# Lending shift adds from VectorE to GpSimd, with two more rules that vary by stretches

## The chip, the cores and the metric

The kernel runs on one core of one Trainium2 chip. The metric is the device time of one execution in microseconds (us); the median of several executions is compared. A profile is one execution recorded by the hardware: busy spans of TensorE (PE, with its weight loads as PEld), VectorE (DVE), ScalarE (ACT) and GpSimd (POOL), the transfers, and what each instruction waited for.

## What is computed

The program is four blocks on a sequence of 2048 rows of 512 numbers: attention, mixer with MLP, attention, mixer with MLP, each with a layer norm before it and a residual sum after it. The attention has 32 query heads of width 16 and one shared key and value head:

```python
def _A_ref(x, wq, wk, wv, wo):
    q = (x @ wq).reshape(B, S, H, Dh).transpose(0, 2, 1, 3)
    k = x @ wk
    v = x @ wv
    scores = jnp.einsum("bhqd,bkd->bhqk", q, k) * (Dh ** -0.5)
    p = _softmax(scores, axis=-1)
    o = jnp.einsum("bhqk,bkd->bhqd", p, v)
    return o.transpose(0, 2, 1, 3).reshape(B, S, H * Dh) @ wo
...
x = x + _A_ref(_layernorm(x, axis=-1), A_wq, A_wk, A_wv, A_wo)
x = x + _B_ref(_layernorm(x, axis=-1), B_w1, B_w2, B_w3, B_w4)
x = x + _A_ref(_layernorm(x, axis=-1), A_wq, A_wk, A_wv, A_wo)
x = x + _B_ref(_layernorm(x, axis=-1), B_w1, B_w2, B_w3, B_w4)
```

The mixer block `_B_ref` normalises, multiplies by w1, applies gelu, shifts four groups of channels by one or two rows up or down, multiplies by w2, and then runs a normalised MLP with w3, gelu and w4. The exponentials are the bulk of the elementwise work: 2 layers of 32 x 2048 x 2048 scores.

## The kernel before

**The work.** Queries are handled in chunks of 512 (the last one of the second layer is cut into two of 256), heads in 8 blocks of four, keys in 16 blocks of 128. A *half* is two heads' scores of one chunk against 128 keys (or, in a chunk of 256, against 256 keys): 1024 columns on 128 partitions, two PSUM banks. There are 2048 halves in all.

**Two ways for a half.** As a *unit* (`declare_unit`, line 1171) PE makes the scores with two matmuls into two neighbouring banks, and ACT writes exp of them to a slot of EA with one instruction (line 1186). As a *pair* (`declare_pair`, line 1194) the same two tiles are evicted by VectorE, one at a time (line 1206): an affine map to uint16 whose bits, read as bfloat16, are close to the exponential. Such an approximation is made three times with different offsets and averaged: the second and third rows come out of the row before by adding a constant to the integers (the *shift add*, line 1243 in `shift_op`), and each of the three rows goes through its own weighted value matmul. J has N_J = 5 slots of three rows.

**The chain of shift adds.** When pair m is declared, one two-row instruction makes the third row of pair m-1 and the second row of pair m (`shift`, line 1224). So each such instruction reads a row that the one before it wrote. Where a block of heads ends with a pair pending, a one-row instruction finishes it (`finish_pair`).

**Who does a shift add.** It is declared for GpSimd if the rows pending there are fewer than ADDS, else for VectorE. When VectorE has nothing to do, `borrow` (line 288) lets it take a ready shift add out of GpSimd's heap, if GpSimd is busy.

**The order.** The whole order of instructions is made in Python by an event-driven plan (`Plan`) with assumed durations. Each engine has a heap of operations; when it comes free, `_pick` takes the ready one with the lowest key of priority and sequence: 0 for unit scores, 1 for VectorE's evictions, 2 for value matmuls and shift adds, 10 for most token work (norms, projections, MLP). The result is a fixed instruction list for each engine, with semaphore waits between them. `assign` (line 1480) decides when a half becomes a pair: only if few pairs are in flight (MAX_PAIRS), VectorE's queue is short (QUEUE), its side work is small (BACKLOG), and a slot of J is free.

**Early score tiles.** `coming` (line 350) computes when ACT will need each unit's scores; they are urgent LEAD (0.4 us) before the last moment, with an allowance for switching PE from another kind of matmul. A unit that isn't urgent yet may be attached to a run of score matmuls that is going on, with the key JOIN (1.3), so ahead of value matmuls (2).

**The clock guess.** The plan assumes that PE runs fast while its recent activity is above a share: WARM (0.40) to get there, STAY (0.36) to stay there (`roll`, line 197). A filler matmul is put in where the activity would fall short of KEEP.

**Stretches.** `temper` (line 1443) sets the rules named in RULES anew each 12.5 us of planned time: digit w of the string TEMPER (116 digits) names one of 16 rows of MOODS.

Of the kernel before, what the change touches and what calls it, by code (L numbers as in the profile page):

```python
# [15 lines left out]
class Late:  # L16
# [4 lines left out]
    def __init__(self, n=1):  # L21
        self.bank = None
        self.n = n
        self.ops = []
        self.gates = []
# [7 lines left out]
class Plan:  # L33
# [12 lines left out]
    WINDOW = 3.4133  # L46
    BINS = 4
    WARM = 0.40
    STAY = 0.36
    KEEP = 0.55  # L50
    CREDIT = 0.2
    URGENT = 0.6
# [6 lines left out]
    PATIENCE = 3.0  # L59
    SLACK = -0.1  # L60
    DMA_LATE = 2.5
    EAGER = 0.0
# [9 lines left out]
    LEAD = 0.4  # L72
    JOIN = 1.3
    LEFT = 1
    HORIZON = 1.0
    LULL = 0.45

    def __init__(self, nc, pool_banks):
        self.nc = nc
# [117 lines left out]
    def roll(self, t):  # L197
        w = int(t * self.BINS / self.WINDOW)
        while self.window < w:
            ask = self.STAY if self.warm else self.WARM  # L200
            self.warm = sum(self.activity[-self.BINS:]) >= ask * self.WINDOW * 2400.0
# [86 lines left out]
    def borrow(self, t):  # L288

        if self.free_at["POOL"] <= t + 1e-9 or self.port - t > self.LULL:  # L290
            return None
# [5 lines left out]
        o.eng, o.dur, o.after = "DVE", o.flex, 0.0  # L297
        return o

    def deferred(self, h, t, joins):  # L300

        low = {}
        if self.pe_kind != "P":
            ps = [o for o in h if o.pe[0] == "P" and o.prio == 2 and o.ready <= t + 1e-9]
            if len(ps) < self.BUNCH and not any(o.ready < t - self.PATIENCE for o in ps):
                low = {o: self.WAITING for o in ps}
        if not (joins and self.pe_kind == "Q"):
            low.update({o: self.ALONE for o in h if o.prio == 0.5})
        return low
# [148 lines left out]
    def run(self, pump):  # L458
        while True:
            if not self.events:  # L460
                if pump(self.now):
                    continue
                break
            t = heapq.heappop(self.events)
            while self.events and self.events[0] <= t + 1e-9:
                heapq.heappop(self.events)
            self.now = max(self.now, t)
            again = True
            while again:
                again = pump(self.now)  # L470
                for e in ENGINES:
                    if self.free_at[e] <= self.now + 1e-9:
                        o = None
                        if e == "PE" and self.now >= self.pe_end - 1e-9 and self.idle():
                            o = self._pick(e, self.now, dense=True)
                            if o is None:
                                self.filler()
                        if o is None:
                            o = self._pick(e, self.now)
                        if o is None and e == "DVE":  # L480
                            o = self.borrow(self.now)
                        if o is None and e == "PE" and self.now >= self.pe_end - 1e-9 and self.left \
                                and self.filler is not None:
                            heapq.heappush(self.events, self.now + 0.25)
                        if o is not None:
                            self._place(o, self.now)
                            again = True
        if self.left:
            for e in ENGINES:
                for o in self.heap[e][:5]:  # L490
                    print("STUCK", e, o.prio, o.seq, o.take)
            raise AssertionError(f"{self.left} operations never became ready at {self.now}")
# [82 lines left out]
def t_x4(n):  # L575
    return 0.068 + n * 0.26e-3
# [18 lines left out]
class Kernel:  # L595
# [13 lines left out]
    ADDS = 6  # L609
# [12 lines left out]
    MAX_PAIRS = 2  # L622
    BACKLOG = 1
    FAR = 20
    FREE = 1
    LONELY = 3
    SOON = 0.45
    QUEUE = 0.7

    STRETCH = 12.5  # L630
    RULES = ("KEEP", "PATIENCE", "BACKLOG", "LONELY", "SOON", "QUEUE", "MAX_PAIRS", "ADDS", "EAGER")
    MOODS = (
        (0.55, 3.0, 1.0, 3.0, 0.45, 0.7, 2, 6, 0.0),
        (0.53, 2.5, 0.8, 3.0, 0.45, 0.7, 2, 7, 0.0),
        (0.57, 3.5, 1.2, 3.3, 0.45, 0.7, 2, 6, 8.0),
        (0.52, 3.0, 1.5, 2.0, 0.6, 0.7, 2, 7, -6.0),
        (0.55, 2.0, 1.0, 3.0, 0.3, 1.0, 2, 6, 0.0),
        (0.55, 4.0, 0.7, 4.0, 0.45, 0.5, 2, 6, 0.0),
        (0.55, 3.0, 1.0, 3.0, 0.45, 0.7, 1, 6, 20.0),
        (0.55, 3.0, 1.5, 2.5, 0.6, 1.0, 3, 7, -15.0),  # L640
        (0.60, 3.0, 0.6, 3.0, 0.2, 0.4, 2, 6, 0.0),
        (0.50, 2.7, 1.1, 2.8, 0.5, 0.8, 2, 6, 0.0),
        (0.55, 3.0, 1.0, 3.0, 0.45, 0.7, 2, 6, 20.0),
        (0.55, 1.0, 1.0, 3.0, 0.45, 0.7, 2, 6, 0.0),
        (0.55, 3.0, 1.0, 3.0, 0.45, 0.7, 2, 7, 0.0),
        (0.55, 3.0, 1.0, 3.0, 0.45, 0.7, 2, 6, -15.0),
        (0.55, 3.0, 1.5, 3.0, 0.7, 1.2, 3, 8, 0.0),
        (0.57, 2.0, 1.0, 2.0, 0.45, 1.0, 3, 6, 0.0),
    )
    TEMPER = "0184777f99f477e52777e374efe430779ef2771778570177e0083e2004000314093e49710fef799feef443873f1e0ee11705c154031407220200"  # L650

    def __init__(self, nc, ins, out):
        self.stretch = -1
# [585 lines left out]
    def shift_op(self, d, f, rows):  # L1239
        n = len(rows)  # L1240
        self.adds = [p for p in self.adds if not p.placed]
        eng = "POOL" if sum(p.weight for p in self.adds) < self.ADDS else "DVE"
        o = self.pl.op(eng, lambda e: e.tensor_scalar(  # L1243
            out=self.J[:, d, :], in0=self.J[:, f, :], scalar1=float(self.STEP), scalar2=1.0, op0=ALU.add, op1=ALU.mult),
            reads=[t for r in rows for t in self.jtag(r - 1)], writes=[t for r in rows for t in self.jtag(r)],
            dur=t_x4(1024 * n) if eng == "DVE" else 0.264 + 0.859 * n, prio=2, side=False, port=True,
            after=0.0 if eng == "DVE" else 0.07)
        if eng == "DVE":
            self.pairs[-1] = o
        else:  # L1250
            o.weight = n
            o.flex = t_x4(1024 * n)
            self.adds.append(o)

    def add_pv(self, g, es, m=None, done=1):
# [187 lines left out]
    def temper(self, now):  # L1443
# [3 lines left out]
        self.stretch = w  # L1447
        mood = self.MOODS[int(self.TEMPER[w], 36) if w < len(self.TEMPER) else 0]
        for name, v in zip(self.RULES, mood):
            setattr(self.pl if hasattr(self.pl, name) else self, name, v)  # L1450

    def pump(self, now):

        self.temper(now)
        did = False
        n = len(self.halves)
        while True:
            if sum(1 for o in self.units[-4:] if not (o.placed and o.end <= now + 1e-9)) >= 3:
                break
            while self.hi in self.given:  # L1460
                self.hi += 1
            self.pl.closing = self.hi + self.CLOSING >= n
            if self.hi >= n:
                break
            self.hi += 1
            self.declare_unit(self.halves[self.hi - 1])
            did = True
        if now > self.attached + self.LONELY and self.assign(now, self.ndve % 2):
            did = True
        if not self.main_done and self.seg == len(self.segs) \  # L1470
                and all(o.placed for o in self.units[-2:]) and self.last_copy.placed:
            self.main_done = self.pl.loose = True
        return did
# [291 lines left out]
```

## Time and profile before

| What | Value |
|---|---|
| median of 3 runs | 1454.44 us (1454.4 to 1456.4) |
| the profiled execution | 1452.62 us, of which 1450.8 us span from the first to the last instruction |
| PE busy | 1425.7 us (98%), 29716 matmuls |
| VectorE busy | 1321.1 us (91%), 2383 instructions |
| ScalarE busy | 1382.0 us (95%), 1471 instructions |
| GpSimd busy | 1139.6 us (79%), 825 instructions |
| shift adds on GpSimd, on VectorE | 529 (967.2 us), 162 (114.7 us) |
| halves as units, as pairs | 1389, 659 |
| transfers | 21.75 MB, 15 GB/s over the span |

How to read it: busy time is the time in which an engine executes an instruction, as a share of the span. Matmuls overlap, so PE's busy share is not its load. In the rows of groups, a line such as "L1243 POOL TENSOR_SCALAR J<-J" names the line of the kernel, the engine, the operation, and what is written from what; then come the shape, the count, the busy us, the mean ns of one, and the engine's idle us just before, with the instructions that ended them.

### The profile page before, as it was taken

The page shows a single profiled execution, that of the slowest core. Times are in us where ns is not written, and L with a number is a line of the kernel's source. Part 1 is how long each engine was busy: PE and PEld are TensorE (multiplying, and loading weights), DVE is VectorE, ACT ScalarE, POOL GpSimd, SP SyncE. Part 2 cuts the span into 40 slices and gives each one's busy share as a digit, 9 for nine tenths or more (in the row PEclk, how much of TensorE's full clock was granted, in tenths as well). Part 3 has the DMA queues.
Part 4 walks back from the last instruction along what each step waited for, and adds up shares of the span by engine and source line. Part 5 has one row for each costly group of instructions (what it writes and reads, how often), then busy time and mean ns, then how long its engine had stood idle before and what let it go on. Part 6 is the DMA issues. An engine that isn't in the chain of part 4 may idle for free.

```text
span 1450.8 us, 65311 instructions
## 1 busy us (share of the span) xinstructions
PE 1425.7 (98%) x29716; PEld 640.2 (44%) x29716; DVE 1321.1 (91%) x2383; ACT 1382.0 (95%) x1471; POOL 1139.6 (79%) x825
## 2 busy tenths in 40 slices
PE   8999999999999999999999999999999999999999
PEld 3343444443444444444444444444434444545565
DVE  8999999999999999999987899999998999988873
ACT  7999999999999999999979999999999999999942
POOL 2889898888978887897855689987798888978841
DMA  6100100001000000010000000100000000000000
GB/s 220 30 6 5 21 6 6 5 6 20 6 5 6 6 7 4 7 20 3 2 3 3 3 10 10 19 8 6 8 11 10 12 6 8 15 13 14 8 15 25
DMA packets 32662, 21.75 MB, mean 15 GB/s; under 512 B 13056, under 2 KB 31872, under 8 KB 32384
## 3 DMA queue, kind: packets, MB, share of 16 engines
q1 hardware_dynamic: 32384, 17.57, 5.2%
q8 instruction: 232, 3.80, 1.0%
q14 instruction: 46, 0.38, 0.1%
HBM read 7.90 MB, written 2.10 MB: 7 GB/s over the span
## 4 chain that ended last, share of the span: by engine, by line
PE 49%; ACT 31%; POOL 10%; DVE 7%; issue 2%; DMA 0%; POOLq 0%
ACT EA L1186 29%; PE PB L1143 16%; PE PB L1298 16%; PE PB L736 15%; POOL J L1243 9%; DVE J L1206 4%; DVE J L1243 1%; ACT G L1698 1%; PE PB L934 1%; POOL SM L870 1%; POOL ZR L1573 1%; DVE ST L850 0%; PE PB L1067 0%; ACT GP L1603 0%; PE PB L991 0%
## 5 line engine op out<-in xcount | busy, mean ns | idle before, releaser
L1186 ACT ACTIVATE EA<-PB 128x1024 bf16<-128x1024 f32 x1389 | 1279.3, 1159 | 11.2 <-PE PB L1143 10.9
L1243 POOL TENSOR_SCALAR J<-J 128x2048 uint16<-128x2048 uint16 (+1 forms) x529 | 967.2, 1828 | 204.6 <-DVE J L1206 95.8
L1206 DVE TENSOR_SCALAR J<-PB 128x512 uint16<-128x512 f32 x1318 | 844.7, 679 | 49.1 <-PE PB L1143 42.5
L1143 PE MATMUL PB<-QT,KT 32*128 32x512 bf16 (+1 forms) x4608 | 592.4, 360 | 8.4 <-ACT EA L1186 4.2
L1298 PE MATMUL PB<-J,VD 128*32 128x256 bf16 (+1 forms) x8880 | 417.3, 264 | 5.5 <-POOL J L1243 2.7
L1298 PE MATMUL PB<-EA,VP 128*32 128x256 bf16 (+1 forms) x6256 | 360.6, 265 | 2.6 <-DVE J L1206 0.6
L1143 PEld LDWEIGHTS PB<-QT,KT 32*128 32x128 bf16 x4608 | 160.4, 91 | 372.5 <-ACT EA L1186 283.8
L1298 PEld LDWEIGHTS PB<-J,VD 128*32 128x32 bf16 x8880 | 188.5, 95 | 145.7 <-issue 96.9
L1298 PEld LDWEIGHTS PB<-EA,VP 128*32 128x32 bf16 x6256 | 147.6, 95 | 146.2 <-issue 129.2
L736 PE MATMUL PB<-ZT,W 128*32 128x512 bf16 (+2 forms) x2816 | 168.8, 342 | 0.0
L1243 DVE TENSOR_SCALAR J<-J 128x2048 uint16<-128x2048 uint16 (+1 forms) x162 | 114.7, 709 | 13.3 <-POOL J L1243 11.8
L736 PE MATMUL PB<-W,G 128*32 128x512 bf16 x1624 | 106.1, 381 | 0.0
L736 PEld LDWEIGHTS PB<-ZT,W 128*32 128x32 bf16 x2816 | 65.9, 96 | 32.7 <-issue 24.7
L1683 DVE CAST G<-PB 128x512 bf16<-128x512 f32 (+2 forms) x126 | 72.0, 578 | 7.8 <-PE PB L736 5.6
L870 POOL TENSOR_TENSOR SM<-SM,MH 128x2 f32<-128x2 f32 (+1 forms) x69 | 54.5, 793 | 21.3 <-DVE SM L872 13.6
L1698 ACT ACTIVATE G<-G 128x1792 bf16<-128x1792 bf16 x29 | 46.9, 1683 | 19.0 <-DVE G L1683 19.0
L736 PEld LDWEIGHTS PB<-W,G 128*32 128x32 bf16 x1624 | 36.5, 96 | 39.2 <-issue 15.0
L1664 POOL TENSOR_TENSOR X<-Y,X 128x512 bf16<-128x512 bf16 x32 | 39.0, 1224 | 14.9 <-DVE Y L1646 13.0
L850 DVE BATCH_NORM_STATS2 ST<-X 128x6 f32<-128x512 bf16 x64 | 42.9, 678 | 1.7 <-DMA X<-in_A_x_dram 1.3
L1338 DVE CAST ACCF<-PB 128x512 bf16<-128x512 f32 (+1 forms) x65 | 39.9, 613 | 1.0 <-PE PB L1298 0.8
L736 PE MATMUL PB<-WO,OT 128*32 128x512 bf16 x512 | 36.9, 382 | 0.1
L736 PE MATMUL PB<-W,GP 128*32 128x512 bf16 x512 | 34.0, 380 | 0.4 <-ACT GP L1603 0.4
(106 smaller groups left out, 716.2 us busy)
## 6 DMA issues: line engine op xcount, KB each, us to landing
OT<-ACCF SPq DMA_DIRECT2D x432, 8.0 KB, 1.8
W<-in_B_w_dram SPq DMA_DIRECT2D x2, 1792.0 KB, 14.8
X<-in_A_x_dram SPq DMA_DIRECT2D x8, 256.0 KB, 5.3
QT<-QS SPq DMA_DIRECT2D x32, 64.0 KB, 2.4
out_dram<-OUTB SPq DMA_DIRECT2D x16, 128.0 KB, 1.7
OT<-ACCF SPq DMA_DIRECT2D x112, 4.0 KB, 2.2
W<-in_B_w_dram SPq DMA_DIRECT2D x2, 512.0 KB, 9.0
WQ<-in_A_wq_dram SPq DMA_DIRECT2D x1, 512.0 KB, 4.9
```

Source lines behind the costliest of these rows:

```text
L736: ins = e.matmul(self.PB[32 * g:32 * g + 32, bank, 0:n], lhsT=lhsT[:, 32 * g:32 * g + 32], rhs=rhs, start=start, stop=stop, tile_position= ...
L850: op("DVE", lambda e, tb=tb: e.bn_stats(self.ST6[:, tb, :], src(tb)), reads=[tagf(tb)], writes=[("ST", tb)], dur=0.606, prio=prio)
L870: op("POOL", lambda e: e.tensor_tensor(out=out, in0=src, in1=self.MH[:, 0, a:b], op=ALU.pow), reads=tags + [("MH",)], writes=tg(r), dur=0. ...
L1143: ins = e.matmul(self.PB[:, bank, j * n:(j + 1) * n], lhsT=self.KT[32 * h:32 * h + 32, la, (kb + j) * 128:(kb + j + 1) * 128], rhs=self.QT ...
L1186: o = q.feeds = op("ACT", lambda e: e.activation(self.EA[:, ea, :, :], self.PB[:, L.bank[0]:L.bank[0] + 2, :], ACTF.Exp, scale=0.25), writ ...
L1206: o = op("DVE", lambda e, i=i, L=L: e.tensor_scalar(out=self.J[:, 3 * s, i * 512:(i + 1) * 512], in0=self.PB[:, L.bank, :], scalar1=128 * ...
L1243: o = self.pl.op(eng, lambda e: e.tensor_scalar(out=self.J[:, d, :], in0=self.J[:, f, :], scalar1=float(self.STEP), scalar2=1.0, op0=ALU.a ...
L1298: ins = e.matmul(self.PB[32 * x:32 * x + 32, A.bank, p * hw:p * hw + hw], lhsT=v[:, la, kb + j, :], rhs=ap[:, i, j * w + u * hw:j * w + u ...
L1338: self.last_copy = op("DVE", lambda e: e.tensor_copy(acc, self.PB[:, A.bank, 0:n]), writes=[ac] + am, dur=t_ps(n), prio=0, side=False, give=A)
L1664: op("POOL", lambda e, tb=tb: e.tensor_tensor(out=self.X[:, tb, :], in0=self.Y[:, tb % 6, :], in1=self.X[:, tb, :], op=ALU.add), reads=[(" ...
L1683: op("DVE", lambda e, f=f, L=L: e.tensor_copy(self.G2[:, f, 0:n], self.PB[:, L.bank, 0:n]), writes=[L] + [(x, f, i) for x in ("G2", "GE") ...
L1698: self.pl.op("ACT", lambda e, i=i: e.activation(self.G2[:, :, i * 128:(i + 1) * 128], self.G2[:, :, i * 128:(i + 1) * 128], ACTF.Gelu_appr ...
```

## The change

It has four parts.

1. `lent` is new: when GpSimd is free and has picked nothing, and VectorE is at work, and the rest of its current instruction plus all operations in its heap of priority 2 or less come to at least CROWD = 1.5 us, GpSimd takes the earliest-declared shift add that is ready in VectorE's heap. The plan then books 1.982 us for a two-row one and 1.123 us for a one-row one. For this, `shift_op` now sets `flex` (VectorE's duration) on every shift add.
2. JOIN and LEAD become two more rules that a stretch sets.
3. The rows 6 and 10 to 13 of MOODS are replaced, all rows get values for JOIN and LEAD (1.3 and 0.4 in the rows that stay), and TEMPER is another string: 99 of its 116 digits differ.
4. STAY is 0.38 instead of 0.36.

```diff
-    STAY = 0.36
+    STAY = 0.38
...
+    CROWD = 1.5
...
+    def lent(self, t):
+
+        if self.free_at["DVE"] <= t + 1e-9 or \
+                self.free_at["DVE"] - t + sum(o.dur for o in self.heap["DVE"] if o.prio <= 2) < self.CROWD:
+            return None
+        h = [o for o in self.heap["DVE"] if o.flex and o.ready <= t + 1e-9]
+        if not h:
+            return None
+        o = min(h, key=lambda o: o.seq)
+        self.heap["DVE"].remove(o)
+        o.eng, o.dur, o.after = "POOL", 1.123 if o.flex < t_x4(1500) else 1.982, 0.07
+        return o
...
                         if o is None and e == "DVE":
                             o = self.borrow(self.now)
+                        if o is None and e == "POOL":
+                            o = self.lent(self.now)
...
-    RULES = ("KEEP", "PATIENCE", "BACKLOG", "LONELY", "SOON", "QUEUE", "MAX_PAIRS", "ADDS", "EAGER")
+    RULES = ("KEEP", "PATIENCE", "BACKLOG", "LONELY", "SOON", "QUEUE", "MAX_PAIRS", "ADDS", "EAGER", "JOIN", "LEAD")
     MOODS = (
-        (0.55, 3.0, 1.0, 3.0, 0.45, 0.7, 2, 6, 0.0),
...
-        (0.55, 3.0, 1.0, 3.0, 0.45, 0.7, 1, 6, 20.0),
...
-        (0.55, 3.0, 1.0, 3.0, 0.45, 0.7, 2, 6, 20.0),
-        (0.55, 1.0, 1.0, 3.0, 0.45, 0.7, 2, 6, 0.0),
-        (0.55, 3.0, 1.0, 3.0, 0.45, 0.7, 2, 7, 0.0),
-        (0.55, 3.0, 1.0, 3.0, 0.45, 0.7, 2, 6, -15.0),
...
+        (0.55, 3.0, 1.0, 3.0, 0.45, 0.7, 2, 6, 0.0, 1.3, 0.4),
...
+        (0.52, 3.0, 1.5, 2.0, 0.6, 0.7, 2, 7, -6.0, 2.5, 0.2),
...
+        (0.55, 3.0, 1.5, 2.5, 0.6, 1.0, 3, 8, -15.0, 2.5, 0.2),
+        (0.55, 3.0, 1.0, 3.0, 0.45, 0.7, 2, 7, 0.0, 2.5, 0.2),
+        (0.55, 3.0, 1.5, 3.0, 0.7, 1.2, 3, 8, 0.0, 2.5, 0.8),
+        (0.57, 2.0, 1.0, 2.0, 0.45, 1.0, 3, 6, 0.0, 0.7, 0.4),
...
-    TEMPER = "0184777f99f477e52777e374efe430779ef2771778570177e0083e2004000314093e49710fef799feef443873f1e0ee11705c154031407220200"
+    TEMPER = "103bc7cc67c9caec87db5774aee9a7acca6dc3a778930a53c8416c8c4b8003305b43bcc7c1dcdb47c5c60877dcca7c5d303a11da72dc1d808000"
...
             after=0.0 if eng == "DVE" else 0.07)
+        o.flex = t_x4(1024 * n)
         if eng == "DVE":
             self.pairs[-1] = o
         else:
             o.weight = n
-            o.flex = t_x4(1024 * n)
             self.adds.append(o)
```

## The prediction

> **What bounds the kernel now.** I read the busy totals first, then the busy time by stretches, the groups of instructions, the waits, and last the timeline of single shifts.
>
> Busy totals say little: every compute engine is above 79%. The table by stretches (span, then busy time and instruction count of each engine, clock, DMA) says more.
>
> ```profile
> core 0: us, PE busy (x) PEld busy (x) DVE busy (x) ACT busy (x) POOL busy (x), PEclk, DMA share, GB/s
> 100.00:750.00 650.00, 639.98 (x12039) 269.96 (x12039) 609.73 (x1059) 648.04 (x690) 550.77 (x388) 1.00 0.04 8
> 750.00:800.00 50.00, 49.47 (x1095) 25.17 (x1082) 41.51 (x90) 40.59 (x41) 24.80 (x23) 1.00 0.01 3
> 800.00:1350.00 550.00, 543.22 (x12096) 246.16 (x12092) 513.41 (x912) 548.37 (x584) 461.10 (x319) 1.00 0.05 10
> 1350.00:1386.00 36.00, 35.70 (x1202) 19.44 (x1194) 32.45 (x60) 35.33 (x39) 28.11 (x19) 1.00 0.04 7
> 1386.00:1450.80 64.80, 61.95 (x1476) 38.96 (x1464) 31.98 (x69) 19.27 (x26) 14.25 (x24) 1.00 0.07 21
> ```
>
> See ACT: 648.04 of 650 and 548.37 of 550, so ScalarE is full wherever attention runs. Only the layer joint (750 to 800) and the last 64.8 us leave it idle. VectorE has 1123.1 of those 1200 us (94%), GpSimd 1011.9 (84%). The granted clock is 1.00 throughout, so it explains nothing.
>
> Who fills these engines (line, engine, operation, tile, shape, count, then busy us, mean ns, idle us before):
>
> ```profile
> L1186 ACT ACTIVATE EA<-PB 128x1024 bf16<-128x1024 f32 x1389 | 1279.3, 1159 | 11.2 <-PE PB L1143 10.9
> L1243 POOL TENSOR_SCALAR J<-J 128x2048 uint16<-128x2048 uint16 x483 | 917.2, 1899 | 173.5 <-DVE J L1206 71.2 <-DVE J L1243 66.2 <-PE PB L1298 5.5
> L1206 DVE TENSOR_SCALAR J<-PB 128x512 uint16<-128x512 f32 x1318 | 844.7, 679 | 49.1 <-PE PB L1143 42.5
> ...
> L1243 DVE TENSOR_SCALAR J<-J 128x2048 uint16<-128x2048 uint16 x144 | 105.9, 736 | 11.5 <-POOL J L1243 10.3
> ```
>
> The 2048 score halves are 1389 exponentials on ACT plus 1318/2 = 659 pairs on VectorE. An exponential occupies ACT for 1279.3/1389 = 0.921 us. The span is therefore: first exponential at 13.5, 1279.3 of exponentials, about 77 of gelus and table loads between them, about 17 idle, and 64.9 after the last one (1385.9 to 1450.8). **The currency is the pair: each further half given to VectorE takes 0.921 us off the end; each one lost adds it.** ACT waits only 10.9 us for scores, so feeding it better is worth at most that.
>
> What limits the pairs? Every two-row shift adds into a row that the shift before it produced, so the 691 shifts form one chain. Counting in the trace, 612 of the 627 two-row shifts had their evicted scores ready before the previous shift ended, typically 9 to 13 us before: five slots of J are full and wait for the chain. A pair comes each (1385-33)/659 = 2.05 us; a link on GpSimd is 1.90 plus some 0.08 between two. So the pair rate hangs on the chain, and the chain is fast only where VectorE does a link (0.69 alone).
>
> **Part 1, the shift lent to GpSimd.** Nothing is removed; a link moves from VectorE to GpSimd if it is ready, GpSimd idle, and VectorE's remaining work at least 1.5 us by the plan. The waits view shows the stall concerned (waiter, releaser, total, times, longest):
>
> ```profile
> POOL J L1243 <- DVE J L1243: 69.8, 69, 3.3
> ...
> ACT EA L1186 <- PE PB L1143: 10.9, 20, 2.0
> ```
>
> The 69.8 us look like the prize, but some 0.69 of each of the 69 is the shift itself being done: 69*0.69 = 48, so only 22 us is time in which the link waited for VectorE. One case, VectorE's timeline and then GpSimd's:
>
> ```profile
> 1128.85 0.69 DVE L943 COPY ZT<-PB 128x1024 bf16<-128x1024 bf16 x1 [0.28 <-PE PB L934]
> 1129.45 1.28 DVE L1206 TENSOR_SCALAR J<-PB 128x512 uint16<-128x512 f32 x2
> 1130.65 0.68 DVE L1243 TENSOR_SCALAR J<-J 128x2048 uint16<-128x2048 uint16 x1
> ```
>
> ```profile
> 1127.45 1.90 POOL L1243 TENSOR_SCALAR J<-J 128x2048 uint16<-128x2048 uint16 x1 [1.31 <-DVE J L1206]
> 1131.42 1.90 POOL L1243 TENSOR_SCALAR J<-J 128x2048 uint16<-128x2048 uint16 x1 [2.07 <-DVE J L1243]
> ```
>
> The shift is ready at 1129.35 and starts at 1130.65, behind two evictions that go first; GpSimd idles 2.07. Lent, it would run on GpSimd from about 1129.4 to 1131.3: the next link starts when it did anyway. **The chain gains nothing; VectorE gains 0.68.** That is the normal case, since break-even is a wait of 1.90 + 0.08 - 0.69 = 1.3 us.
>
> How many? Of the 162 shifts on VectorE, 22 stood ready with GpSimd idle for over 0.45 us; 12 for over 1. I take 20. Freed: 20*0.69 = 13.8 us. A pair costs VectorE 2*844.7/1318 = 1.28 plus its share of shifts, 114.7/659 = 0.17 (the 114.7 is all 162 shifts): 1.46. All of it turned into pairs gives 9.5. Or the freed time borrows other links from GpSimd: 20 links at 1.2 saved are 24 us of chain, at 2.05 a pair 11.7. Both need the other resource too, so I take about half, **5 pairs: -4.6 us**. Ends: -10.8 (11.7 pairs), and +8 (rival A). GpSimd's price, 20*1.9 = 38 us, lies in idle time: it has 188 idle us in the 1200. If that cover failed, its other work (normalisation powers, residual adds) would start up to 1.9 later, and these feed the token work, which has slack until a chunk ends.
>
> **The rule that speaks against it.** First the row (VectorE's shifts: minimum, median and maximum ns):
>
> ```profile
> L1243 DVE TENSOR_SCALAR J<-J x162: 416/693/1458, 45.2 to 1387.9; 128x2048 uint16<-128x2048 uint16 x144, 128x1024 uint16<-128x1024 uint16 x18
> ```
>
> The longest, 1458, shows that something can hold a shift up, but the median is the undisturbed 693, and the excess over 0.69 of all 144 two-row shifts sums to only 7.3 us. VectorE's queue in the case above holds evictions from PSUM, which ran at 0.64 each beside GpSimd's 1.90. The rule is in the Trainium skill, "SBUF — State Buffer", section "SBUF: two separate sides": VectorE and GpSimd share a pair of ports under an exclusive lock, and whichever comes second blocks for the whole instruction. By the rule at its worst, a lent shift holds VectorE's next ported operation for 1.90 us: 20*1.9 = 38 us lost, far more than the 13.8 gained. By the row, 7.3/144 = 0.05 each, 20 lent shifts cost 1 us. I take the row.
>
> The same skill, "GPSIMD Engine Reference", section "Performance versus the Vector engine", puts GpSimd at about twice VectorE's time for elementwise work. By 2 a lent link would cost 1.38 and the chain would win 0.5 each time (20*0.5 = 10 us, 5 more pairs); by the rows it is 1.90/0.69 = 2.75 and the gain is nil. The row decides again.
>
> **Part 2, the stretches.** Each stretch of 12.5 planned us picks one of 16 sets of rules; 99 of the 116 digits change, so nearly the whole order is redrawn. Averaged over the digits, the limit on shifts pending for GpSimd goes from 6.60 to 6.94, pairs in flight from 2.40 to 2.50, backlog from 1.17 to 1.22. All three admit a little more pair work. With J's slots already full, I give them the smaller share: **-2 us (2 pairs)**. No row shows a redrawn order. Ends: if order alone recovered a tenth of VectorE's 77 idle us, 7.7/1.46 = 5 pairs, -5; if it lost as much, +5.
>
> **Part 3, early score tiles.** JOIN is 2.5 in 42 stretches (an early tile then yields to ready value products) and 0.7 in 9; LEAD is 0.8 in 22 and 0.2 in 20. An early tile is put in before ACT needs it. The nearest row is ACT's 10.9 us, 20 waits. I take **-1 us**; ends -5 (half of these waits gone) and +14 (the 20 stretches of LEAD 0.2 hold 250 us, some 270 exponentials, each 0.05 late).
>
> **Part 4, STAY 0.36 to 0.38.** The plan's guess of when the clock stays high becomes more cautious. With 1.00 granted in every stretch, no wait changes: 0. Its own fillers (67 of about 0.2 us of PE) cost ACT nothing now.
>
> The head (13.5) and the last 64.9 us keep their work. Sum: -4.6 - 2 - 1 = -7.6. The profiled execution took 1452.62 (span 1450.8 and 1.8 around it): 1445.0. The median shown is 1454.44, 1.8 above; on it the sum is 1446.8. I say **1447**.
>
> **The rivals.**
>
> A, slower: *the link grows*. Place: the chain. The queue that is tested counts all ready operations of the scores, not only those that would go before the shift, and its own 0.6 is among them; so a link is lent when it would have waited only about 0.9. Price: 1.98 - 0.9 - 0.69 = 0.4 each. With 20 lent that is 8 us of chain, 4 pairs, +3.6, about what is gained; it decides from some 45 lent on: 45*0.4 = 18 us, 9 pairs, +8: **1463**. For it: 612 of 627 links are chain-bound. Against it: only 22 of 162 shifts qualified by the trace. Chance 0.20.
>
> B, slower: *scores come late*. The later urgency and the yielding early tiles cost ACT as worked out in part 3: +14 less half of part 1's gain, about **1466**. For it: 42 stretches yield. Against it: PE bunching in before left just 10.9 us. Chance 0.10.
>
> C, *nothing nets*: the lent shifts are few, since 106 of the 162 shifts started within 0.5 us of being ready, and VectorE's time goes idle for want of free slots: **1454**. Chance 0.12. That the rule never fires belongs here.
>
> D: *the order frees far more*: VectorE's 77 idle us shrink by a fifth as well (10 pairs) on top of part 1: 16 to 20 pairs, -15 to -18: **1438**. For it: GpSimd has 188 us idle. Against it: full slots. Chance 0.13.
>
> The forecast, 1443 to 1451, has 0.45.
>
> **How the numbers follow.** About 0.2% (2.9 us) is what a measurement here can tell from no change. The forecast and D lie mostly below 1451.5: 0.58. Between 1451.5 and 1457.3: most of C and edges of others: 0.12. A and B: 0.30. The range 1437 to 1463 holds the forecast, C, most of D and half of A and B. The forecast's own range is 1443 to 1451.
>
> **What would show it.** The exponentials fall from 1389 to about 1381 and the evictions rise from 1318 to about 1334: that is the main sign. VectorE's shifts fall below 162 with GpSimd's above 529, and GpSimd's wait for VectorE's shift falls from 69.8 us by some 20. ACT's wait for scores stays near 11; at 25 or more B is right. Under A the exponentials are more than 1389 although VectorE's shifts fell. The forecast is wrong if the count of exponentials doesn't move.

## The result, and the profile after

The changed kernel takes 1449.28 us (median of 6 runs, 1447.0 to 1449.96) against 1455.0 us (6 runs, 1453.9 to 1456.4): the ratio is 0.9958, with a 95% interval of 0.9945 to 0.9971. That is 5.7 us faster, where 7.6 were forecast, and inside the forecast's own range. But the sign that the forecast called the main one points the other way. First the groups of the page of the changed kernel (count, then busy us, mean ns, idle us before):

```profile
L1202 ACT ACTIVATE EA<-PB 128x1024 bf16<-128x1024 f32 x1391 | 1281.3, 1159 | 7.2 <-PE PB L1159 6.5
L1259 POOL TENSOR_SCALAR J<-J 128x2048 uint16<-128x2048 uint16 (+1 forms) x532 | 975.3, 1833 | 186.9 <-DVE J L1222 88.9
L1222 DVE TENSOR_SCALAR J<-PB 128x512 uint16<-128x512 f32 x1314 | 844.9, 682 | 49.2 <-PE PB L1159 43.7
...
L1259 DVE TENSOR_SCALAR J<-J 128x2048 uint16<-128x2048 uint16 (+1 forms) x165 | 114.7, 696 | 12.9 <-POOL J L1259 11.0
```

The exponentials rose from 1389 to 1391, so there are two pairs fewer, not eight more (the forecast's own sum has seven). VectorE's shift adds rose from 162 to 165 although the plan lent 18: in the plan, `borrow` took 128 instead of 104. Two rows of the waits view of the changed kernel (waiter, releaser, total us, times, longest):

```profile
POOL J L1259 <- DVE J L1259: 51.9, 58, 2.1
...
ACT EA L1202 <- PE PB L1159: 6.5, 9, 1.5
```

GpSimd's wait for a shift on VectorE fell by 18 us, and ACT's wait for scores from 10.9 to 6.5. Now the busy time of the engines, split at 1385 us, just before the last exponential ends (PE, PEld, DVE, ACT, POOL, then clock, DMA share, GB/s); the kernel before:

```profile
0.00:1385.00 1385.00, 1362.73 (x28220) 600.63 (x28224) 1288.38 (x2314) 1361.77 (x1445) 1124.47 (x801) 1.00 0.06 15
1385.00:1450.80 65.80, 62.95 (x1500) 39.59 (x1492) 32.71 (x70) 20.25 (x27) 15.16 (x25) 1.00 0.07 21
```

and the changed one:

```profile
0.00:1385.00 1385.00, 1364.84 (x28222) 601.70 (x28222) 1286.33 (x2318) 1364.37 (x1447) 1137.51 (x805) 1.00 0.06 15
1385.00:1447.60 62.60, 59.39 (x1422) 35.99 (x1422) 28.93 (x64) 19.68 (x27) 12.60 (x24) 1.00 0.07 22
```

By 1385 us VectorE has done 2318 instructions in 2.1 us less time, and has 64 left instead of 70. What those are, ACT's timeline shows after the last exponential; before:

```profile
1385.96 1.28 ACT L1603 ACT_TABLE_LOAD   x1
1393.96 1.06 ACT L1603 ACTIVATE GP<-GP 128x1024 bf16<-128x1024 bf16 x1 [6.72 <-DVE G L1683]
```

after:

```profile
1385.35 1.28 ACT L1619 ACT_TABLE_LOAD   x1
1390.98 1.06 ACT L1619 ACTIVATE GP<-GP 128x1024 bf16<-128x1024 bf16 x1 [4.34 <-DVE G L1699]
```

ACT's first gelu waits for the evictions of the up-projection (G). Before, eight of them were still to be made after the last exponential; now it is four. From this gelu to the end of the span both take about the same (56.8 and 56.6 us).

So the span of the two profiled executions, 1450.8 and 1447.6, is 3.2 us shorter: 2.0 more of exponentials, 2.7 less idle time of ACT between the first and the last of them (17.2 to 14.6), which with small differences puts the last exponential's end 0.6 earlier, and 2.6 less behind it. The medians differ by 5.7, because the profiled execution before (1452.62) lay 2.4 below its median; that rest is in neither trace.

### The profile page after: what moved, and what is told of

Read it like the earlier page. It is cut to its first block, busy times and chain, and to the rows that moved or that the text cites. A ratio compares the mean times of both kernels' runs of the same rounds, so it can differ in the third digit from the quotient of the medians.

```text
span 1447.6 us, 65153 instructions
## 1 busy us (share of the span) xinstructions
PE 1424.2 (98%) x29644; PEld 637.7 (44%) x29644; DVE 1315.3 (91%) x2382; ACT 1384.1 (96%) x1473; POOL 1150.1 (79%) x828
## 4 chain that ended last, share of the span: by engine, by line
ACT 55%; PE 36%; POOL 6%; DVE 2%; issue 1%; DMA 0%; POOLq 0%
ACT EA L1202 53%; PE PB L752 13%; PE PB L1159 11%; PE PB L1314 11%; POOL J L1259 4%; DVE J L1222 1%; ACT G L1714 1%; PE PB L950 1%; ACT GP L1619 1%; POOL SM L886 1%; POOL ZR L1589 0%; ACT L1202 0%; PE PB L1007 0%; DVE ST L866 0%; ACT L1619 0%
## 5 line engine op out<-in xcount | busy, mean ns | idle before, releaser
L1314 PE MATMUL PB<-J,VD 128*32 128x256 bf16 (+1 forms) x8820 | 408.2, 264 | 5.9 <-POOL J L1259 3.4
L1314 PE MATMUL PB<-EA,VP 128*32 128x256 bf16 (+1 forms) x6276 | 356.8, 264 | 2.3 <-ACT EA L1202 0.6
L1740 DVE TENSOR_TENSOR OUTB<-PB,X 128x512 bf16<-128x512 f32 x16 | 11.0, 689 | 27.3 <-PE PB L752 27.3
```

The lines of the kernel that those rows point to most:

```text
L1314: ins = e.matmul(self.PB[32 * x:32 * x + 32, A.bank, p * hw:p * hw + hw], lhsT=v[:, la, kb + j, :], rhs=ap[:, i, j * w + u * hw:j * w + u ...
```

## The experiments

All runs are timed against the kernel before. The changed kernel was run once more beside them.

> The changed kernel once more, as the reference for the three runs beside it. Every theory: ratio to before 0.9945 to 0.9971, 1391 exponentials.

Measured: 1449.14 us, ratio 0.9957 (0.9944 to 0.9969), 1391 exponentials, span 1446.9. This trace is the reference below; its waits differ little from those shown above (GpSimd for VectorE's shifts 52.1 us, ACT for scores 7.0).

### Undoing one part and letting the plan draw the order again

Four kernels change one thing each, and the plan does the rest:

```diff
# never lent (changed kernel)
-    CROWD = 1.5
+    CROWD = 1e9
# JOIN and LEAD fixed (changed kernel), in each row of MOODS
-        (0.55, 3.0, 1.5, 3.0, 0.7, 1.2, 3, 8, 0.0, 2.5, 0.8),
+        (0.55, 3.0, 1.5, 3.0, 0.7, 1.2, 3, 8, 0.0, 1.3, 0.4),
# lent alone (kernel before): CROWD, lent(), its call in run() and flex as in the change; MOODS, TEMPER and STAY stay
# one digit (kernel before)
-    TEMPER = "0184777f
+    TEMPER = "1184777f
```

> The changed kernel with CROWD so large that nothing is ever lent; the plan draws the whole order anew under the changed string. The loan theory: 18 loans lost, 5 to 10 us slower than the changed kernel, 1454 to 1460 us. The order theory: the string is fitted digit by digit to one course of the plan, and any departure from it loses the fit: over 4% slower than before, above 1510 us, with 20 or more additional exponentials.

> The changed kernel with JOIN 1.3 and LEAD 0.4 in all rows, as before the change, the order drawn anew under the changed string. If these two rules have only their own small effect: within 1% of the changed kernel, 1440 to 1465 us. If the string fits only the course it was made for, as with the loans: above 1500 us, 20 or more additional exponentials.

> The kernel before with only the loan added (rules, rows and string as before), the order drawn anew. The loan theory: faster than before by 3 to 8 us, 1446 to 1452 us. The order theory: above 1500 us with 20 or more additional exponentials, although shifts are lent.

> The kernel before with only the first digit of its string changed from 0 to 1: no rule is added or removed. The order theory: as slow as the two runs beside it, above 1500 us. The loan theory says nothing of it; if a part's own effect explains the other two, this stays within 1% of before, 1440 to 1470 us.

| Kernel | median us | ratio (95%) | exponentials | ACT waits for scores, us | mean granted clock |
|---|---|---|---|---|---|
| never lent | 1536.38 | 1.0561 (1.054 to 1.0582) | 1415 | 33.7 | 0.992 |
| JOIN and LEAD fixed | 1539.28 | 1.0589 (1.0558 to 1.062) | 1424 | 28.6 | 0.992 |
| lent alone | 1512.39 | 1.0396 (1.0377 to 1.0415) | 1424 | 21.6 | 0.997 |
| one digit | 1518.87 | 1.0441 (1.0422 to 1.046) | 1417 | 25.9 | 0.996 |

The groups of the one-digit kernel, which adds and removes no rule:

```profile
L1186 ACT ACTIVATE EA<-PB 128x1024 bf16<-128x1024 f32 x1417 | 1306.5, 1136 | 27.0 <-PE PB L1143 25.9
L1243 POOL TENSOR_SCALAR J<-J 128x2048 uint16<-128x2048 uint16 (+1 forms) x497 | 910.6, 1832 | 296.5 <-DVE J L1206 181.3 <-DVE J L1243 68.5 <-PE PB L1298 10.0
```

The reader is to see 28 more exponentials than in the kernel before, 92 us more idle time of GpSimd before its shifts, and more waiting of ACT. Its span grows by 66.4, nearly all of it in three terms: 28*0.921 = 25.8 from the pairs lost, 33.7 from more idle time of ACT between exponentials (17.2 to 50.9), and 6.4 behind the last one (64.9 to 71.3). A single digit costs 4.4%, where a part undone or added costs 4.0 to 5.9%, so these runs do not price any part. They are what one expects if each string fits one course of the plan, and they show what leaving that course costs; on that the order theory is right. What the loans are worth inside their course has to be asked in another way.

### Moving the loans alone, with the order kept

To price the loans, the order must stand. After the plan has run, a few operations are put on the other engine at a given moment, and all else keeps its place; the waits are then made from the dependencies as always. This method serves all kernels of this section:

```diff
             self.pl.run(self.pump)
+            self.give_back()
...
+    def reseat(self, moved):
+        for e in ("DVE", "POOL"):
+            ops = [o for x in ("DVE", "POOL") for o in self.pl.order[x] if o.eng == e]
+            moved[e] = sorted(ops, key=lambda o: (o.start, o.seq))
+        for e in ("DVE", "POOL"):
+            self.pl.order[e] = moved[e]
+            for i, o in enumerate(moved[e]):
+                o.pos = i
...
+    def give_back(self):
+        for o in self.pl.gone:
+            o.eng = "DVE"
+        self.reseat({})
```

(`gone` is the list of the operations that `lent` took.)

> The changed kernel with its order kept, except that the 18 lent shift adds go back to VectorE, each right behind the instruction that VectorE is at when GpSimd would take it. The loan theory: VectorE has 18*0.69 = 12.4 us more to do and most of the gain is lost, ratio 0.998 to 1.003. The order theory: each link of the chain ends about 1.2 us earlier and VectorE is held 0.69, which cancels; within 2 us of the changed kernel, ratio 0.994 to 0.998.

Measured: 1455.69 us, ratio 1.0004 (0.9994 to 1.0014), 6.5 us over the changed kernel beside it. Nearly the whole gain is gone with the 18 loans, still at 1391 exponentials. Three rows of its waits:

```profile
POOL J L1278 <- DVE J L1241: 110.8, 72, 6.8
...
POOL J L1278 <- DVE J L1278: 67.1, 65, 3.2
...
ACT EA L1221 <- PE PB L1178: 10.4, 22, 1.5
```

GpSimd waits 67.1 us for VectorE's shifts (51.9 with the loans), ACT 10.4 for scores (6.5). Counting from exponential to exponential against the reference, the delay grows in small steps to 6.3 us at the last one: 0.35 for each loan. The order theory, which had 2 us at most, is wrong here. So is the chain as the cause: given back, the 18 links became shorter. From the end of the last eviction or shift that a link reads (by the plan's dependencies, with the times of the traces) to its own end, they take 1.24 us in the mean, in the reference 2.13. The chain won 0.9 us a loan and the kernel still lost.

Was it VectorE's time, or that the evictions were held up behind the shift? In a variant the shift goes behind the ready evictions:

```diff
+            for p in [p for p in self.pl.order["DVE"] if o.start < p.start < use]:
+                if p.prio > 1 or p.ready > o.start + 0.1:
+                    break
+                o.start = p.start + 1e-6
             o.eng = "DVE"
```

(`use` is the start of the first operation that reads the result.)

> The 18 shift adds given back to VectorE, but behind the evictions that stand ready at that moment (0 to 1.1 us later by the plan), which is where VectorE's own priorities put them. If VectorE's time is the price: as slow as when they went first, ratio 0.9995 to 1.002. If the loss came from holding up evictions: half of it is gone, ratio 0.997 to 0.999.

Measured: 1459.71 us, ratio 1.0037 (1.0024 to 1.0051). That is not less, but more than with the shifts in front. That doesn't rule the held-up evictions out, though: most of this delay is of another kind, the fallen clock described below, and without it 3.6 us are left in the trace against 6.3. Whether a part of the loss came from held-up evictions stays open.

Then the loans stay on GpSimd, and VectorE gets 18 idle instructions of the same length:

```diff
+        for t in times:
+            o = self.pl.op("DVE", lambda e: e.bn_stats(self.SCR, self.ONES), reads=[("ONES",)], writes=[("SCR",)],
+                           dur=0.69, side=False)
+            o.start, o.end, o.placed = t, t + 0.69, True
+            self.pl.order["DVE"].append(o)
```

> The changed kernel with its order and its loans kept, and 18 additional idle instructions of 0.68 us on VectorE (statistics of a constant row into scratch that nobody reads), one at each moment of a loan. The chain of shift adds is not touched. If what the loans give is VectorE's time: about as slow as with the shifts given back, ratio 1.000 to 1.002, 5 to 9 us over the changed kernel. If giving back lost through the chain or through GpSimd's place in the order: within 2 us of the changed kernel, ratio below 0.9975.

> As the one before, but each of the 18 instructions stands midway between two loans. If VectorE's time has one price everywhere: the same as at the loans, 5 to 9 us over the changed kernel. If only the crowded moments cost, because elsewhere VectorE's idle time takes them in: 0 to 4 us over the changed kernel, ratio 0.9955 to 0.9985.

Measured: at the loans 1458.72 us, ratio 1.0034 (1.0021 to 1.0048); between them 1453.73 us, ratio 0.9994 (0.9986 to 1.0003), 4.6 over the reference. So 18*0.68 = 12.2 us of VectorE's time, with no shift moved, costs 9.6 and 4.6 us, where giving the shifts back cost 6.5. **In this order, VectorE's time is what the loans give.** Between the loans it costs less, slightly under the 5 us that one price everywhere would have and above the 4 us of the other case.

The idle instructions at the loans cost 9.6 us, beyond the upper edge that was expected. The profiled execution is the slowest of its seven (1463.12 us, 14.4 over that of the reference). The table by stretches says where; first the reference, then the kernel with the idle instructions:

```profile
120.00:130.00 10.00, 10.00 (x175) 4.23 (x171) 9.65 (x17) 10.00 (x12) 8.96 (x5) 1.00 0.02 4
130.00:140.00 10.00, 9.96 (x169) 3.99 (x161) 9.93 (x18) 10.00 (x12) 8.63 (x5) 1.00 0.03 6
```

```profile
120.00:130.00 10.00, 8.45 (x110) 3.13 (x110) 8.28 (x12) 7.46 (x9) 7.52 (x6) 0.78 0.01 2
130.00:140.00 10.00, 10.00 (x149) 3.44 (x145) 8.37 (x15) 8.15 (x9) 4.74 (x3) 0.71 0.04 8
```

The granted clock, third from the right, falls to 0.78 and 0.71, and ACT is busy 7.46 and 8.15 of 10 us instead of all of it. A second such dip follows at 260 us. Over the two stretches the last exponential's delay grows by 5.0 and 3.5 us, of 13.8 in all; the rest is 5.3. The variant with the shifts behind the evictions dips at the same two places (4.8 and 3.5 of 11.9; rest 3.6), the one between the loans once, near 970 us (2.4 of 6.2; rest 3.8), and the one with the shifts in front not at all (6.3). Without the dips, the 0.68 us on VectorE costs 0.2 to 0.35 us at the end, in these four traces. The dips are not the same in each execution: with the idle instructions at the loans, the mean granted clock of the seven was 0.994 to 0.999, and with the shifts in front one of eleven had 0.995 (1461.88 us).

Now the other direction, into the kernel before: shifts that stood ready on VectorE while GpSimd was idle are moved to GpSimd.

```diff
+        for o in self.pl.order["DVE"]:
+            if o.flex is None or o.start - o.ready < 0.85:
+                continue
...
+            if t + 0.85 > o.start or following < t + 0.6:
+                continue
+            o.start, o.eng = t, "POOL"
```

(`t` is the moment when the shift is ready and GpSimd free; `following` is GpSimd's next start. In the second kernel the bounds are 0.1, 0.1 and 0.3.)

> The kernel before with its order kept, except that 7 shift adds which stood ready for over 0.85 us while GpSimd was idle are lent to it at that moment. The loan theory: 7*0.69 = 4.8 us off VectorE, 2 to 4 us faster, ratio 0.997 to 0.9985. The order theory: the later instructions stay where they are, so nothing uses the time; within 1.5 us, ratio 0.999 to 1.001.

> As the one before, but 30 shift adds are lent, nearly all with waits far below the 1.3 us of break-even. The loan theory: 30*0.69 = 20.7 us off VectorE, at least 5 us faster, ratio below 0.9965. Rival A (the link grows): 30 links longer by 0.4 to 1.2 us, 12 to 36 us of chain of which half is taken up by slack, 6 to 18 us slower, ratio 1.004 to 1.012. The order theory: the five slots of J absorb the longer links, within 3 us, ratio 0.998 to 1.002.

Measured: with 7 loans 1456.18 us, ratio 1.001 (1.0002 to 1.0019); with 30 loans 1476.92 us, ratio 1.0153 (1.0139 to 1.0167), slower even than the upper end that was expected under rival A. Rows of the waits with 30 loans:

```profile
ACT EA L1213 <- PE PB L1170: 25.0, 43, 2.0
...
POOL J L1270 <- DVE J L1270: 38.1, 49, 1.0
```

GpSimd's wait for VectorE's shifts, the apparent prize, has fallen from 69.8 to 38.1, and the kernel is 21 us slower: ACT waits 25.0 us for scores instead of 10.9. The last exponential ends 21.1 us late, 0.70 for each loan, at an unchanged 1389. By the same count as above, the 30 links grew from 1.38 to 2.04 us, 0.66 each: a loan whose wait is far below 1.3 us lengthens the chain, as rival A had it. The 7 links with long waits kept their length (2.02 and 1.98 us), and the 4.8 us that VectorE was spared brought nothing in an order that was not drawn for them. The kept orders thus price VectorE's time only where it is taken away; of the two that give it, neither gains.

### One step that might beat both

The gelu that waits in the timeline above covers two things: the last mixer's (GP) and the up-projection's (G). The first needs no G:

```diff
-               reads=gt + ([("G2", f, x) for f in range(14) for x in range(4)] if kept else []), writes=gt,
+               reads=gt + ([("G2", f, x) for f in range(14) for x in range(4)] if kept and not last else []), writes=gt,
...
+            if o in self.held and not self.closing:
+                continue
```

(`last` marks the last chunk but one of the second layer; `held` keeps that gelu back until attention closes.)

> The changed kernel, whose order is kept up to the end of attention; there the mixer's gelu of the third-last stretch of tokens no longer waits for the last evictions of the up-projection (it is taken as soon as the last exponentials are placed), so TensorE can run that mixer product in the gap that is now filled. If the last evictions alone set the end, nothing moves: ratio 0.9945 to 0.9971 as for the changed kernel. If the product was late because of the gelu, 1 to 2 us less: ratio 0.993 to 0.9955.

```profile
1385.19 1.06 ACT L1623 ACTIVATE GP<-GP 128x1024 bf16<-128x1024 bf16 x1
1389.24 4.87 ACT L1720 ACTIVATE G<-G 128x1792 bf16<-128x1792 bf16 x3 [3.00 <-DVE G L1705]
```

ACT's timeline shows the first gelu 4 us ahead of the others, as intended. Measured: 1448.21 us, ratio 0.9954 (0.9941 to 0.9968). From the last exponential to the end it takes 61.1 us, the reference 61.8. The intervals overlap almost wholly; whether the 0.9 us of the medians is real stays open. It is the fastest median of all runs.

## Why the prediction was right, and where it was not

**What bounds the kernel.** ACT is still full in attention (the fourth busy time in the row below, 649.11 of 650 us after the change, 648.04 before):

```profile
100.00:750.00 650.00, 642.37 (x12115) 271.75 (x12110) 610.75 (x1072) 649.11 (x690) 556.77 (x393) 1.00 0.04 8
```

But "the currency is the pair" was too narrow: the gain came with two pairs fewer. The step that failed is the term that turned freed time into pairs (5 of the loan and 2 of the stretches, 6.6 of the 7.6 us): these were -2 pairs, 2.0 us more of exponentials, and in their place stand 2.7 us less idle time of ACT and 2.6 us less behind the last exponential. For the latter the forecast had nothing ("the last 64.9 us keep their work"). That the sum came out near the measured 5.7 us is therefore luck in good part: the size was right, and most of the way to it was not.

VectorE's time has three buyers: pairs, the token work that must be done before the last gelus, and scores that reach ACT in time. The second and third got more in the changed kernel. That the loans paid for them is in part inferred. With the loans given back, ACT is idle for 19.1 us between its exponentials instead of 15.2, but from the last exponential to the end it takes 62.1 us and in the reference 61.8; so the shorter end came with the redrawn order, and is not tied to the loans by any run.

A reading behind the pairs was wrong too. The forecast had 612 of the 627 two-row shifts bound by the shift before, with their scores evicted 9 to 13 us earlier. By the plan's dependencies and the times of the trace they are 526, the evictions are typically 0.9 to 2.9 us ahead, and for 101 shifts the eviction by VectorE ended last, 139 us later in all. The waits say the same, before and after the change:

```profile
POOL J L1243 <- DVE J L1206: 95.8, 76, 12.7
```

```profile
POOL J L1259 <- DVE J L1222: 88.9, 69, 6.6
```

So the chain alone does not set the rate of pairs.

**Part 1, the loan.** The count was right (20 forecast, 18 lent by the plan), and so was that the loan gives VectorE's time and not a faster chain: idle instructions alone undo most of it or more (4.6 and 9.6 us). The price was 4.6/20 = 0.23 us each; the order-kept runs gave 0.2 to 0.35, and 6.5 us for all 18 against -4.6. This is an upper estimate, since that order was drawn around the loans. GpSimd's wait for VectorE's shifts fell by 18 us, as said (some 20). That VectorE's shifts would fall below 162 was wrong: `borrow` filled the freed time. The factor of two that the forecast weighed against its rows is measured in the Trainium skill, "GPSIMD Engine Reference", section "Performance versus the Vector engine", for an addition of two f32 inputs; this operation has one input of uint16, and the rows' 2.75 was the right one to take.

**The port rule against the row.** Taking the row was right in sum, but it looked at the shifts alone. Other operations of VectorE are held as well, already in the kernel before:

```profile
L887 DVE TENSOR_SCALAR ZR<-Y,MV,SM x32: 395/408/1854, 255.3 to 1419.1; 128x512 bf16<-128x512 bf16 x32
```

The longest starts 0.19 us after a shift on GpSimd and ends 0.15 us after it. Counting all of VectorE's instructions that took over 1.3 times the median of their kind, the time above the median is 21.9 us (42 instructions) before and 17.9 us (30) after: with the loans it did not grow. In the order with 18 idle instructions, an operation met GpSimd's shift and was held for all of it, as the Trainium skill's "SBUF — State Buffer", section "SBUF: two separate sides", says of the one that comes second; by the starts in the profile, though, VectorE's operation came first. VectorE and then GpSimd, with the idle instructions at the loans:

```profile
261.06 2.13 DVE L926 TENSOR_SCALAR ZR<-Y,MV,SM 128x512 bf16<-128x512 bf16 x1
```

```profile
261.15 1.90 POOL L1282 TENSOR_SCALAR J<-J 128x2048 uint16<-128x2048 uint16 x1
```

and the same two operations in the reference:

```profile
254.26 0.41 DVE L903 TENSOR_SCALAR ZR<-Y,MV,SM 128x512 bf16<-128x512 bf16 x1
```

```profile
254.42 2.00 POOL L1259 TENSOR_SCALAR J<-J 128x2048 uint16<-128x2048 uint16 x1
```

0.16 us apart, VectorE's 0.41 goes through and GpSimd's shift takes 2.00; 0.09 us apart, it takes 2.13 and ends 0.14 us after GpSimd's 1.90. The second clock dip begins some 4 us later.

**Part 2, the stretches.** The -2 us and its bounds of 5 on either side came from averages over the digits, and were of the wrong kind: one digit moved the kernel by 4.4%. With the loans given back, the new order stands at 1.0004, so the stretches and the early tiles show no gain of their own in it; but that order was drawn with the loans.

**Part 3, early tiles.** ACT's wait for scores fell by 4.4 us, near the good end (-5) rather than the -1 taken. Rule and loan are not separated by this: giving the loans back alone raised the wait to 10.4.

**Part 4, STAY.** As forecast, nothing: with 0.36 in the changed kernel, the plan draws the same instruction lists on every engine, so it is the same program.

**The rivals.** A's price is real (0.70 us each in the run with 30, at an unchanged number of pairs), but the change lends 18, below its point of 45. Its sign came only by half: there are more exponentials, but VectorE's shifts did not fall, and the kernel is faster. B fell: the wait sank. C and D fell with the measured ratio.

**What stays open.** Whether a string fitted to the old rules with the same effort would reach the same time: the loan helps in the order drawn for it, but no run tells a better rule from a better fit.

## What to carry to other kernels

Where a plan or a search has fitted an order, undoing one part and drawing the order anew prices the fit, not the part; to price a part, keep the order and move only its operations, or put idle instructions of the same length where they stood. In an order that was drawn for the part this is an upper price. An engine's freed time may be spent on another kind of work than the one that looks like the currency, so forecast the places where the engines meet at the end, and not one count. And a wait that is mostly the other engine's useful work is no prize: here some 48 of 69.8 us were the shift itself (the forecast's estimate), and more loans made the wait shorter and the kernel slower.

## What the runs showed of the hardware

Two things were unexpected. First, a stretch of VectorE with one idle instruction of 0.68 us more cost up to 5 us. With the idle instructions at the loans, VectorE and then PE show:

```profile
122.41 2.01 DVE L1282 TENSOR_SCALAR J<-J 128x1024 uint16<-128x1024 uint16 x1
```

```profile
124.48 0.29 PE L1337 MATMUL PB<-J,VD 128*32 128x256 bf16 x4 [0.99 <-DVE J L1282]
```

The one-row shift took 2.01 us (0.65 in the reference), PE stood for 0.99 us waiting for it, and the granted clock was then 0.56, 0.50 and 0.91 in the three stretches of 5 us from 125 to 140 us. The sequence is shown; that the stop alone lowers the clock is not. With 30 loans PE stood for 1.70 us at 144 us and the clock fell to 0.66 in the next 5 us, but it also stood for 1.19 us at 244 us, and there the clock stayed at 1.00. That it halves agrees with the Trainium skill, "TensorE: Matmul & The Clock Gate", section "Part 1: The HAM clock gate", which has two states, full and half rate, set by recent activity. Second, which of two operations comes first on the shared ports was decided within 0.1 us or so, with 1.7 us at stake for VectorE (2.13 against 0.41, in the two cases shown, at starts 0.09 and 0.16 us ahead of GpSimd's).
